# Even rounds of scores and sums, loads in pieces, and one tile for a pair's keys and queries

## The chip, the cores and the metric

The kernel runs on one core of a Trainium2 chip. The metric is the device time of one launch in microseconds (us). Names of engines: PE is TensorE's matmuls and PEld its weight loads, ACT is ScalarE, DVE is VectorE, POOL is GpSimd, SP is SyncE, which here only issues DMA transfers.

## The reference

Sigmoid attention and then a mixture of experts with one expert for each token:

```python
# q, k, v: 8 batches, 12 heads, 448 tokens, 64 wide
scores = (1 / sqrt(64)) * q @ k.T - log(448)
attn   = sigmoid(scores)
x      = attn @ v                      # tokens x 768 after the heads are put side by side
# 3584 tokens, 8 experts of 768 -> 1024 -> 768
logits = x @ w_gate;  e = argmax(logits);  g = softmax(logits)[e]
out    = g * (relu(x @ w1[e]) @ w2[e])
```

There is no softmax over the keys, so the score of each key can be activated and summed by itself.

## The kernel before

**Attention.** Two heads make a pair (`g`, 48 of them, six to a batch), and two pairs are worked on together (`u = g // 2`). The 448 keys are seven chunks of 64. One step `s` is one chunk of two pairs, so there are 168 steps, seven to each `u`. `scores(s)` issues four matmuls of 64 keys by 448 queries, one to each 64x64 quarter of PE (the profile records two passes for each, so eight records), and then two activations on ACT (`squash`, line 748) that write the activated scores to tiles `at`, of which there are eight buffers. Their PSUM tiles (`ps_sc`) are four, two a step. `weighted(s)` issues the four matmuls that sum a chunk's values by its activated scores; the seven chunks of a pair accumulate in one PSUM tile.

**Rounds.** Up to step 70 (`START`) attention runs alone. At each even step the loop at line 940 first issues sums (`weigh_to`), then gating work of earlier batches (`stages_early`), then the token transposes of pairs whose sums are done (`turn_tokens`), then two steps of scores (`score_to`), then the copies of finished pairs (`copy_tokens`). Before the change the sums go up to step s-2, but never over the end of a `u`:

```python
weigh_to(min(s - 1, (done_av // ST + 1) * ST))
```

As a `u` has seven steps and a round has two, the rounds at steps 16, 30, 44 and 58 have one sum, and those at 18, 32, 46 and 60 have three. Step 70 has three. `summed` notes the round in which a `u` was finished; a batch's gate matmuls (`gate_a`, line 289, 128x32 form) follow one round later, when its third `u` is done.

From step 70 on, the MoE's matmuls (128x128 form) are interleaved, and a `u`'s seven steps of scores and sums come as one burst. Order on each engine is the program's (`manual_schedule`).

**Start.** Pairs 0 and 1 are loaded with their rows on the partitions (`load_rows`, line 673), pair 0 from SP and pair 1 from ACT, and transposed on PE (`turn_rows`, line 702) behind a warm-up of 33 matmuls: all seven chunks of the queries of both pairs, then those of the keys, whose first chunk has a PSUM tile of its own so that step 0 can begin early. DVE and ACT copy the results. Pair 3 is loaded in the same way from ACT and transposed on DVE in 32x32 blocks (`turn_blocks`, line 724): eight instructions for its keys and eight for its queries. Pair 2 and all later ones are loaded in pieces of 128 bytes and transposed by one DVE instruction each (`turn`, line 694). Behind pair 3's blocks, DVE makes a constant (line 101) and transposes pair 2. Scores of pairs 2 and 3 begin at step 7.

`blank_records` (line 109) fills a table in DRAM that the later gating writes into: two fills on POOL and one DMA from a tile of the ring `wst`, whose five buffers later hold raw weights.

Of the kernel before, what the change touches and what calls it, by code (L numbers as in the profile page):

```python
# [18 lines left out]
P = 128  # L19
# [5 lines left out]
def tile_sigmoid_attention_top1_moe(  # L25
# [83 lines left out]
    def blank_records():  # L109
        blank = wpool.tile([P, 1024], U32, tag="wst", bufs=RAWS_AHEAD, name="blank")  # L110
        blank3 = blank[:, : E * NT // P * 2].rearrange("p (r w) -> p r w", w=2)
        for w, val in enumerate((int(BIG), 0)):
            nc.gpsimd.iota(blank3[:, :, w], pattern=[[0, E * NT // P]], base=val, channel_multiplier=0)
        nc.gpsimd.dma_start(recs.rearrange("(p r) w -> p r w", p=P), blank3)
# [542 lines left out]
    def load_pair(g):  # L657
# [3 lines left out]
        for nm, src in (("k", k), ("q", q)):  # L661
# [8 lines left out]
                    )  # L670
            ops[g, nm + "n"] = t

    def load_rows(g, nm):

        t = apool.tile([P, KC, D], F32, tag=nm + "n", bufs=4, name=f"{nm}n_{g}")
        src = (k if nm == "k" else q)[0, 2 * g : 2 * g + 2]
        (nc.scalar if g else nc.sync).dma_start(t, src.rearrange("h (p c) d -> (h p) c d", c=KC))
        ops[g, nm + "n"] = t

    def load_values(g):  # L680
        if g >= NG or (g, "v") in ops:
# [39 lines left out]
                if to > at:  # L721
                    copy(t[:, at * DK : to * DK], ps[:, at * DK : to * DK])

    def turn_blocks(g, nm):

        rows = ops.pop((g, nm + "n"))
        t = apool.tile([P, S], F32, tag=nm + "t", bufs=4, name=f"{nm}t_{g}")
        for a in range(0, P, DK):
            for p in (0, 32):
                for d in (0, 32):  # L730
                    nc.vector.transpose(
                        t[a + d : a + d + 32].rearrange("d (c p) -> d c p", c=KC)[:, :, p : p + 32],
                        rows[a + p : a + p + 32, :, d : d + 32],
                    )
        ops[g, nm] = t

    def warm_up(n):

# [79 lines left out]
    START = 70  # L818
    LOADS = (START - 15, START - 12, START - 9, START - 7, START - 5)
    FIRST = (START - 3, START - 1, START - 1)  # L820
    SPLITS = (START - 11, START - 10, START - 9, START - 8, START - 4, START - 3)
    PB = NP // 2 * ST
    MIX = (7, 7)

# [3 lines left out]
        2: lambda u: (turn(2 * u + 3, "k"), load_pair(2 * u + 5)),  # L828
        3: lambda u: (turn(2 * u + 3, "q"), load_values(2 * u + 3)),
    }  # L830
    BURST = 4

    def attention():

        order = ExitStack()
        order.enter_context(tc.manual_schedule())
        make_identity(nc, ident)
        warm_up(WARM)
        for nm in "qk":
            load_rows(0, nm)  # L840
            load_rows(CROSS, nm)
        for n in range(2):
            load_values(n)
        for nm in "kq":
            load_rows(3, nm)
        turn_rows("q", 0)
        turn_rows("k", 1)
        for nm in "kq":
            turn_blocks(3, nm)
        nc.gpsimd.memset(wg, 0.0)  # L850
        nc.gpsimd.dma_start(wg[:, :, :E], w_gate.rearrange("(t p) e -> p t e", p=P))
        setup()
        load_pair(2)
        blank_records()
        for n in (2, 3):
            load_values(n)
        list_constants()
        done_av = done_sc = 0

        def weigh_to(n):  # L860
            nonlocal done_av
            while done_av < min(n, N_ST):
                weighted(done_av)
                done_av += 1

        def score_to(n):
            nonlocal done_sc
            while done_sc < min(n, N_ST):
                scores(done_sc)
                done_sc += 1  # L870

        gate = {}

        def stage(what, b):
            g = gate.setdefault(b, {})
            if what == "B":
                g["oh"], g["z"] = early_b()
            elif what == "C":
                ri, *g["early"] = early_c(g["oh"], g["z"])
                g["c"] = None, None, ri  # L880
            elif what == "C3":
                oh, ce, keep, cnt, sums = g["early"]
                g["lm"] = early_c2(oh, ce, keep, cnt)
                early_c3()
            elif what == "D":
                oh, ce, keep, cnt, sums = g["early"]
                for n in range(2):
                    sl_of[n] = early_d(n, g["lm"][:, n], sums[:, :, n], cnt[:, n * E : (n + 1) * E])
            elif what == "b":
                g["oh"], g["z"] = gate_b(b)  # L890
            elif what == "c":
                g["c"] = gate_c(b, g["oh"], g["z"])
            elif what == "c2":
                g["lm"] = gate_c2(b, g["oh"], *g["c"])
            elif what == "c3":
                gate_c3(b, *g["c"][:2])
            elif what == "l" and b > 0:
                load_slot(b - 1, g["c"][2])
            elif what == "d":
                sl_of[b] = gate_d(b, g["lm"])  # L900
            elif what[0] == "s":
                gate_d2(b, int(what[1]))
            elif what == "g" and b > 0:
                gate_g(b - 1)
            elif what == "e" and b > 0:
                gate_e(b - 1)

        LATE = {8: "b", 10: "c", 11: ("l", "c2"), 12: "c3", 15: "d", 16: "g", 26: "e"}
        FOUR = ("s0", "s1", "s2", "s3")
        PUTS = tuple(dict(zip(range(r, r + 8, 2), FOUR)) for r in (START - PB, START + 10 - 2 * PB)) + 4 * (dict(zip((27, 28, 29, 30), FOUR)),)  # L910
        PUTS += (dict(zip((25, 26, 27, 28), FOUR)), {9: "s0", 10: "s1"})
        LAST = {3: "b", 5: "c", 6: ("l", "c2"), 7: "c3", 8: "d", 9: "g"}
        EARLY = {5: "B", 7: "C", 9: ("l", "C3"), 11: "D", 13: "g", 32: "e"}
        FIRST_LATE = {8: "b", 10: "c", 11: ("l", "c2"), 12: "c3", 15: "d", 16: "g", 26: "e"}
        PLACES = {}
        for b in range(B):
            places = ({}, EARLY, FIRST_LATE, LATE, LATE, LATE, LATE, LAST)[b]
            for r, what in [*places.items(), *PUTS[b].items()]:
                at = (b + 1) * PB + r
                at += at < START and at % 2  # L920
                PLACES.setdefault(at, []).extend((w, b) for w in ((what,) if isinstance(what, str) else what))

        summed = {}

        def stages_early(s):
            for b in range(B):
                if summed.get((b + 1) * NP // 2 - 1) == s - 2:
                    gate_a(b)
            for w in PLACES.get(s, ()):
                stage(*w)  # L930

        def stages_late(s):
            u, i = divmod(s, ST)
            b, r = divmod(s - PB, PB)
            if r == (BURST if b < B - 1 else 1) and (b + 1) * PB >= START:
                gate_a(b)
            for w in PLACES.get(s, ()):
                stage(*w)

        for s in range(N_ST + 11):  # L940
            u, i = divmod(s, ST)
            a = u * ST
            if s in LOADS:
                wts.load(LOADS.index(s) + 1)
            if s in FIRST:
                wts.ahead(FIRST.index(s) + 1)
            if s < START:
                if s % 2 == 0:
                    weigh_to(min(s - 1, (done_av // ST + 1) * ST))
                    if done_av and done_av % ST == 0:  # L950
                        summed.setdefault(done_av // ST - 1, s)
                    stages_early(s)
                    turn_tokens()
                    score_to(s + 2 if s else LEAD + 1)
                    copy_tokens()
            elif s == START:
                weigh_to(a)
                turn_tokens()
                score_to(a + 2)
                copy_tokens()  # L960
            yield s, MIX[0]
            keep_tokens()
            if s >= START:
                b, r = divmod(s - 3 * PB, PB)
                b += 1
                stages_late(s)
                if i == BURST:
                    for n in range(ST):
                        score_to(a + n + 3)
                        weigh_to(a + n + 1)  # L970
                        turn_tokens()
                        if n == ST - 1:
                            copy_tokens()
                        if r == PB - ST + BURST and n < KD:
                            split_tokens(b, n, nc.scalar.copy if n in (1, 4) else nc.vector.tensor_copy)
            if i in READY and s < N_ST:
                READY[i](u)
            if s in SPLITS:
                split_tokens(0, SPLITS.index(s), nc.vector.tensor_copy)
            yield s, MIX[1]  # L980
        keep_tokens()
        order.close()
# [384 lines left out]
```

## Time and profile before

| | us |
|---|---|
| median of 3 runs | 771.38 (771.14 to 772.06) |
| the profiled execution | 771.24, span 769.4 |
| PE busy | 762.8 (99%) |
| ACT, DVE, POOL busy | 382.2, 378.2, 349.1 |
| TensorE's granted clock | 1.00 |

The span runs from the first instruction of the program to the last. PE's busy time says little of how well its four quarters are filled: a matmul counts as busy until its modelled end. The weight loads (PEld) tell when each matmul's turn comes, four to a wave while the 64x64 quarters are in use. A bracket in a timeline row is the engine's idle time before the row and what ended it; "issue" means that the profile shows no one it waited for.

### The profile page before, as it was taken

What the parts mean: (1) busy time and instruction counts of PE and PEld (TensorE: products, weight loads), DVE (VectorE), ACT (ScalarE), POOL (GpSimd) and SP (SyncE); (2) the same over time, 40 slices, a digit from 0 to 9 for tenths busy, and PEclk for the clock granted to TensorE, in tenths of its full rate; (3) what the DMA queues carried; (4) which work ended last, traced back from release to release, by engine and by line L of the source; (5) the groups of instructions that cost most, each with busy time, mean ns of one, the idle gap of its engine ahead of it and who ended that gap; (6) DMA issues with size and microseconds to landing.
All of it is one profiled execution on the core that took longest, in us unless ns stands there. A gap on an engine that the chain in (4) does not pass through costs nothing. (4 is left out here: it accounts for less than half of the span.)

```text
span 769.4 us, 15492 instructions
## 1 busy us (share of the span) xinstructions
PE 762.8 (99%) x5585; PEld 589.3 (77%) x5585; DVE 378.2 (49%) x790; ACT 382.2 (50%) x686; POOL 349.1 (45%) x342
## 2 busy tenths in 40 slices
PE   9999999999999999999999999999999999999997
PEld 5655547678687696876967769678689999999996
DVE  5433678375253751628415474244746392244443
ACT  6878676644526545364344552545523333445451
POOL 8665526245353151531705407044266654764351
PEclk9999999999999999999999999999999999999999
DMA  9786898896678665694575966566087454656671
GB/s 231 166 180 148 177 243 177 189 217 149 157 162 192 147 154 120 160 242 99 134 184 110 218 149 168 129 185 151 24 217 173 142 142 107 204 154 172 199 222 38
DMA packets 309921, 125.67 MB, mean 163 GB/s; under 512 B 208158, under 2 KB 305358, under 8 KB 309840
## 3 DMA queue, kind: packets, MB, share of 16 engines
q1 hardware_dynamic: 303632, 112.19, 61.6%
q0 software_dynamic: 5632, 11.53, 5.4%
q8 instruction: 45, 0.74, 0.5%
q10 hardware_dynamic: 576, 0.92, 0.4%
q14 instruction: 36, 0.29, 0.1%
HBM read 102.49 MB, written 22.49 MB: 162 GB/s over the span
## 5 line engine op out<-in xcount | busy, mean ns | idle before, releaser
L750 ACT ACTIVATE at<-sc,bias_s 128x448 f32<-128x448 f32 x336 | 190.7, 633 | 106.9 <-PE sc L768 106.2
L162 POOL TENSOR_TENSOR w1l<-wst,w1h 128x768 fp32r<-128x768 f32 x72 | 132.8, 1852 | 210.5 <-ACT w1h L161 207.9
L162 POOL TENSOR_TENSOR w2l<-wst,w2h 128x512 fp32r<-128x512 f32 x84 | 106.9, 1296 | 134.7 <-ACT w2h L161 134.6
L768 PE MATMUL sc<-qt,kt 64*64 64x448 f32 x1344 | 162.0, 543 | 0.0
L784 PE MATMUL av<-at,vn 64*64 64x448 f32 x1344 | 160.1, 536 | 0.0
L243 PE MATMUL ps<-xh,w1h 128*128 128x448 f32 x336 | 124.3, 370 | 0.0
L243 PE MATMUL ps<-xh,w1l 128*128 128x448 f32 x336 | 123.3, 367 | 0.0
L243 PE MATMUL ps<-xl,w1h 128*128 128x448 f32 x336 | 123.3, 367 | 0.0
L266 PE MATMUL ps<-hh,w2l 128*128 128x448 f32 x336 | 123.3, 367 | 0.0
L266 PE MATMUL ps<-hl,w2h 128*128 128x448 f32 x336 | 123.2, 367 | 0.0
L266 PE MATMUL ps<-hh,w2h 128*128 128x448 f32 x336 | 122.6, 365 | 0.0
L768 PEld LDWEIGHTS sc<-qt,kt 64*64 64x64 f32 x1344 | 75.3, 188 | 59.0 <-issue 46.5
L784 PEld LDWEIGHTS av<-at,vn 64*64 64x64 f32 x1344 | 57.5, 133 | 64.0 <-issue 53.8
L161 ACT CAST w2h<-wst 128x512 fp32r<-128x512 f32 x108 | 64.5, 620 | 75.7 <-PE ps L266 63.3
L250 ACT ACTIVATE hh<-ps 128x448 fp32r<-128x448 f32 x56 | 30.5, 545 | 138.1 <-PE ps L243 125.3
L279 DVE TENSOR_TENSOR ps<-ps,gt 128x448 f32<-128x448 f32 x42 | 40.7, 970 | 87.0 <-PE ps L266 84.7
L612 DVE STREAM_TRANSPOSE xt<-av 128x448 f32<-128x448 f32 x45 | 26.5, 626 | 95.3 <-PE av L784 95.3
L251 DVE SCALAR_TENSOR_TENSOR hl<-ps,hh 128x448 fp32r<-128x448 f32 x56 | 34.4, 614 | 76.5 <-ACT hh L250 67.0
L243 PEld LDWEIGHTS ps<-xh,w1h 128*128 128x128 f32 x336 | 63.1, 188 | 9.4 <-issue 4.4
L266 PEld LDWEIGHTS ps<-hh,w2l 128*128 128x128 f32 x336 | 65.2, 194 | 6.6 <-issue 3.5
L266 PEld LDWEIGHTS ps<-hl,w2h 128*128 128x128 f32 x336 | 65.2, 194 | 6.2 <-issue 3.2
L266 PEld LDWEIGHTS ps<-hh,w2h 128*128 128x128 f32 x336 | 65.2, 194 | 3.2
(215 smaller groups left out, 916.5 us busy)
## 6 DMA issues: line engine op xcount, KB each, us to landing
wst<-in_moe_w_dram SPq DMA_DIRECT2D x72, 384.0 KB
wst<-in_moe_w_dram SPq DMA_DIRECT2D x54, 512.0 KB
x_tok<-xt SPq DMA_DIRECT2D x64, 168.0 KB
qn<-in_q_dram SPq DMA_DIRECT2D x180, 56.0 KB
raw<-x_tok SPq DMA_DIRECT2D x28, 336.0 KB
out_dram<-ob SPq DMA_DIRECT2D x84, 112.0 KB
kn<-in_k_dram SPq DMA_DIRECT2D x104, 56.0 KB
kn<-in_k_dram POOLq DMA_DIRECT2D x76, 56.0 KB, 4.1
```

The lines of the kernel that those rows point to most:

```text
L161: nc.scalar.copy(hi, st)
L162: eng.tensor_tensor(lo, st, hi.bitcast(F32), op=ALU.subtract)
L243: nc.tensor.matmul(ps[:, :S], a[:, ws], b_, start=(t == 0 and n == 0), stop=(t == KD - 1 and n == 2))
L250: nc.scalar.activation(hh[:, :S], ps[:, :S], AF.Relu)
L251: nc.vector.scalar_tensor_tensor(hl[:, :S], ps[:, :S], 0.0, hh[:, :S].bitcast(F32), op0=ALU.max, op1=ALU.subtract)
L266: nc.tensor.matmul(ps[:, :S], a, b_, start=(j == 0 and n == 0), stop=(j == KF - 1 and n == 2))
L279: nc.vector.tensor_tensor(by_gate, by_gate, gate_rows[b], op=ALU.mult)
L612: nc.vector.transpose(xts[b][:, :, t, :], pv[:, :S].rearrange("p (j s) -> p j s", s=32))
L750: nc.scalar.activation(at, ps[:, :S], AF.Sigmoid, bias=bias_s, scale=SCALE)
L768: nc.tensor.matmul(ps[quarter(g, h), :S], ks, ops[g, "q"][own], start=True, stop=True)
L784: nc.tensor.matmul(psv[g][OWN[1 - h if g == CROSS else h], :S], ops[g, "v"][rows, c, :], at[rows], start=(c == 0), stop=(c == KC - 1))
```

## The change

Five things. (1) Sums go up to step s-3 (`BEHIND = 2`) with no stop at the end of a `u`, so each round from step 4 to step 68 has two sums and step 70 has four; a `u` may now be finished in the middle of a round, and `summed` notes it in that round. (2) `load_rows` issues two transfers for each of the four tiles: chunks 0 to 3 (1024 bytes a partition) and chunks 4 to 6 (768 bytes). (3) Pair 3's keys and queries lie side by side in one tile of the ring `wst`, still one transfer each, both from ACT; their transposes go to a second such tile by eight instructions that each take keys and queries together. (4) `blank_records` is issued at step 14, not at the start. (5) The last of the six splits of the first slot's tokens (`SPLITS`) is at step 68, not 67.

```diff
+    def rows_of(g, nm):
+        return (k if nm == "k" else q)[0, 2 * g : 2 * g + 2].rearrange("h (p c) d -> (h p) c d", c=KC)
+
     def load_rows(g, nm):
         t = apool.tile([P, KC, D], F32, tag=nm + "n", bufs=4, name=f"{nm}n_{g}")
-        src = (k if nm == "k" else q)[0, 2 * g : 2 * g + 2]
-        (nc.scalar if g else nc.sync).dma_start(t, src.rearrange("h (p c) d -> (h p) c d", c=KC))
+        for cs in (slice(0, 4), slice(4, KC)):
+            (nc.scalar if g else nc.sync).dma_start(t[:, cs], rows_of(g, nm)[:, cs])
         ops[g, nm + "n"] = t
+
+    def load_both(g):
+        t = wpool.tile([P, 1024], F32, tag="wst", bufs=RAWS_AHEAD, name=f"kqn_{g}")
+        ops[g, "kqn"] = t = t[:, : 2 * S].rearrange("p (n c d) -> p n c d", n=2, c=KC)
+        for n, nm in enumerate("kq"):
+            nc.scalar.dma_start(t[:, n], rows_of(g, nm))
...
-    def turn_blocks(g, nm):
-        rows = ops.pop((g, nm + "n"))
-        t = apool.tile([P, S], F32, tag=nm + "t", bufs=4, name=f"{nm}t_{g}")
+    def turn_blocks(g):
+        rows = ops.pop((g, "kqn")).rearrange("p n c d -> p (n c) d")
+        t = wpool.tile([P, 1024], F32, tag="wst", bufs=RAWS_AHEAD, name=f"kqt_{g}")[:, : 2 * S]
+        by_c = t.rearrange("d (c p) -> d c p", p=DK)
         for a in range(0, P, DK):
             for p in (0, 32):
                 for d in (0, 32):
-                    nc.vector.transpose(
-                        t[a + d : a + d + 32].rearrange("d (c p) -> d c p", c=KC)[:, :, p : p + 32],
-                        rows[a + p : a + p + 32, :, d : d + 32],
-                    )
-        ops[g, nm] = t
+                    nc.vector.transpose(by_c[a + d : a + d + 32, :, p : p + 32], rows[a + p : a + p + 32, :, d : d + 32])
+        ops[g, "k"], ops[g, "q"] = t[:, :S], t[:, S:]
...
-    SPLITS = (START - 11, START - 10, START - 9, START - 8, START - 4, START - 3)
+    SPLITS = (START - 11, START - 10, START - 9, START - 8, START - 4, START - 2)
...
-    BURST = 4
+    BURST, BEHIND = 4, 2
...
-        for nm in "kq":
-            load_rows(3, nm)
+        load_both(3)
...
-        for nm in "kq":
-            turn_blocks(3, nm)
+        turn_blocks(3)
...
         load_pair(2)
-        blank_records()
...
-                    weigh_to(min(s - 1, (done_av // ST + 1) * ST))
-                    if done_av and done_av % ST == 0:
-                        summed.setdefault(done_av // ST - 1, s)
+                    weigh_to(s - BEHIND)
+                    while len(summed) < done_av // ST:
+                        summed[len(summed)] = s
...
+            if s == 2 * ST:
+                blank_records()
             yield s, MIX[0]
```

## Rows read from the trace of the kernel before

**Rows 1.** The page: busy time, share of the span, instructions.

```profile
PE 762.8 (99%) x5585; PEld 589.3 (77%) x5585; DVE 378.2 (49%) x790; ACT 382.2 (50%) x686; POOL 349.1 (45%) x342
```

**Rows 2.** Timeline of PEld: start, duration, instruction, count, idle before; even stretches.

```profile
88.75 1.35 PEld L768 LDWEIGHTS sc<-qt,kt 64*64 64x64 f32 x16 [0.20 <-issue]
...
96.27 0.17 PEld L784 LDWEIGHTS av<-at,vn 64*64 64x64 f32 x4
...
143.98 0.15 PEld L784 LDWEIGHTS av<-at,vn 64*64 64x64 f32 x4 [0.22 <-issue]
144.84 0.19 PEld L243 LDWEIGHTS ps<-xh,w1h 128*128 128x128 f32 x1 [0.70 <-issue]
```

**Rows 3.** PEld by stretches: window, length, busy (loads), clock, DMA share, GB/s.

```profile
6.45:42.53 36.08, 21.24 (x376) 1.00 0.87 187
43.81:77.48 33.67, 17.26 (x352) 1.00 0.75 161
86.00:110.64 24.64, 12.39 (x256) 1.00 0.98 209
111.91:120.72 8.81, 4.53 (x88) 1.00 0.89 184
134.09:144.83 10.74, 5.00 (x112) 1.00 0.72 147
```

**Rows 4.** Timeline of ACT around step 16.

```profile
27.86 3.98 ACT L750 ACTIVATE at<-sc,bias_s 128x448 f32<-128x448 f32 x7 [0.80 <-PE sc L768]
```

**Rows 5.** Timeline of PEld behind step 16.

```profile
30.32 0.20 PEld L768 LDWEIGHTS sc<-qt,kt 64*64 64x64 f32 x2 [0.21 <-ACT at L750]
30.33 0.14 PEld L784 LDWEIGHTS av<-at,vn 64*64 64x64 f32 x2
```

**Rows 6.** Timeline of PEld at the end of the second stretch.

```profile
76.65 0.14 PEld L784 LDWEIGHTS av<-at,vn 64*64 64x64 f32 x2 [0.24 <-issue]
77.50 0.91 PEld L294 LDWEIGHTS psg<-xf,wg 128*32 128x32 f32 x24 [0.71 <-issue]
```

**Rows 7.** Timeline of the start, SP and PEld.

```profile
1.17 0.44 SPq L677 DMA_DIRECT2D kn<-in_k_dram  x1
...
1.04 3.30 PEld L741 LDWEIGHTS <-ones 128*128 128x128 bf16 x33 [1.04 <-DVE ones L76]
4.55 0.94 PEld L714 LDWEIGHTS turn_q<-ident,qn 64*64 64x64 f32 x56 [0.22 <-issue]
5.54 0.21 PEld L714 LDWEIGHTS sc_first_k<-ident,kn 64*64 64x64 f32 x8
...
6.46 0.21 PEld L768 LDWEIGHTS sc<-qt,kt 64*64 64x64 f32 x8
```

**Rows 8.** All engines by stretches of the start; last columns clock, DMA share, GB/s.

```profile
2.00:4.00 2.00, 2.00 (x21) 2.00 (x20) 0.00 (x0) 0.63 (x2) 2.00 (x6) 1.00 0.87 293
4.00:6.00 2.00, 1.93 (x91) 1.73 (x93) 0.35 (x1) 0.29 (x1) 2.00 (x5) 1.00 1.05 399
6.00:8.00 2.00, 2.00 (x57) 1.02 (x52) 1.76 (x6) 1.36 (x4) 1.69 (x5) 1.00 1.11 311
```

**Rows 9.** Waits of SP's queue up to 10 us: total, times, longest.

```profile
SPq L667 <- DMA qn<-in_q_dram: 1.9, 1, 1.9
```

**Rows 10.** Timeline of DVE behind the start.

```profile
10.44 3.32 DVE L731 STREAM_TRANSPOSE qt<-qn 32x224 f32<-32x224 f32 x8
13.79 0.29 DVE L101 TENSOR_SCALAR upper<-step_i,slot 128x128 bf16<-128x128 f32 x1
...
14.58 0.60 DVE L699 STREAM_TRANSPOSE qt<-qn 128x448 f32<-128x448 f32 x1
```

**Rows 11.** Timeline of ACT: the first activations.

```profile
7.48 4.30 ACT L750 ACTIVATE at<-sc,bias_s 128x448 f32<-128x448 f32 x8 [0.32 <-PE sc L768]
```

**Rows 12.** Timeline of POOL: the blank records' issue, and the idle time before step 16.

```profile
6.93 0.60 POOL L114 DMA_DIRECT2D recs<-blank  x1 [0.30 <-POOL blank L113]
...
29.56 0.57 POOL L687 DMA_DIRECT2D vn<-in_v_dram  x1 [4.56 <-PE av L784]
```

## The prediction, made before the changed kernel was run

> **What bounds the kernel now.** I read the busy table first: TensorE (PE) is busy 762.8 us of a span of 769.4 [rows 1]. So only what moves PE's own idle time can move the end; the other engines, at about half, matter where PE waits for them. The row doesn't show such waits, because a pipelined matmul counts as busy while two of the four tiles stand still. So I went to the weight loads (PEld), each of which begins one matmul. In the attention part PE works as four 64x64 tiles, and four loads make a wave. In an undisturbed stretch 20 waves take from 88.75 to 96.27, or 0.376 us each [rows 2]. One step (scores or sums of two pairs, eight loads) is two waves, 0.752 us.
>
> The stretches table then gives the loss: window, less loads / 4 x 0.376 [rows 3]. Stretch 1 (6.45 to 42.53): 36.08 - 94 x 0.376 = 0.74. Stretch 2 (43.81): 33.67 - 88 x 0.376 = 0.58. Stretch 3 (86.00): 24.64 - 64 x 0.376 = 0.58. Stretch 4 (111.91): 8.81 - 22 x 0.376 = 0.54. A burst after step 70 (134.09): 10.74 - 28 x 0.376 = 0.21. [...] 0.21 is what a stretch pays to fill and drain. The first four lose 0.53 + 0.37 + 0.37 + 0.33 = 1.60 us more. Each of them holds one or two uneven rounds: steps 16; 30 and 44; 58; and at step 70 three sums behind two.
>
> How an uneven round costs: in step 16's round one sum stands where two did, so PE is at its scores 0.75 us sooner, while ScalarE (ACT) is still in seven activations without a pause [rows 4]. Scores have four PSUM tiles, two steps' worth, so they wait for ACT, and PE comes out of it with two tiles in scores and two already in sums [rows 5]. From there one half runs a wave ahead of the other. It costs nothing until the stretch ends: then the last loads come as two, not four, and PE drains half empty. Stretch 2 ends so, with two loads at 76.65; the burst ends with four at 143.98; both then need 0.85 us to the next form of matmul [rows 2, 6]. Half a wave pair late is 0.376 us, which is the 0.33 to 0.37 counted.
>
> **The change, part by part.** *Even rounds.* Every round before step 70 now has two sums, of steps s-4 and s-3 in the running count, so PE spends 1.50 us before each pair of scores, as it does today in the rounds without a loss. Step 70 has four sums; the last one's activations get one sum (0.75 us) more. The matmuls are the same in number. Four steps of activated scores are held instead of three, which is all eight buffers; the slot that is written was freed by a sum two steps of PE's order earlier (sum s-4, sum s-3, scores s), so no wait. The token copies and the values' reloads come up to one round (1.5 us) later for half of the pairs, behind them on GpSimd (POOL) and SyncE (SP) the next keys and queries; these are used seven steps (10.5 us) on. If that cover went, PE would wait for keys by what is over. I take 1.60 us saved of stretches 1 to 4, between 0 (the loss is the drain's own) and 1.60, nearest to the burst's 0.21.
>
> *Loads in two pieces.* Today the queries' transposes start at 4.55, 0.21 after the warm-up's last load ends (1.04 + 3.30), and end at 5.49; the keys' at 5.54, and the first score is at 6.46 [rows 7]. The keys' transposes take 0.92. With pieces, four sevenths of each can be done before the second piece is there, so the order is PE's own: 0.94 + 0.92 from about 4.4 gives 6.26, 0.2 us sooner. Above this the gain could be 0.4 (three sevenths of 0.92 behind the last keys at 5.5, less the copies); below it nothing, if smaller descriptors stretch the stream: 917 KB in four tiles at 399 GB/s [rows 8] take 2.3 us, and a tenth more would eat the 0.2. I take 0.2.
>
> Every DMA issue counts: four more, 0.44 us each on SP, and as many on ACT, which has nothing else to do before the copies at 5.6. What is queued behind them shows on SP: its next transfer waited 1.9 us for the first queries' landing [rows 9]. It is the ninth of SP and ACT together, so eight are in flight and the next waits. Now q and k alone are eight, so the values of pairs 0 and 1 and the fourth pair's loads wait for the first pieces, about 3.8, and flow when the keys are through (0.3 MB of the 917 KB remain at 4.0, so 4.8). The stream has hardly a gap. The values are now needed one round later, behind four steps of scores: 6.26 + 4 x 0.752 = 9.3; that they are there by 8.2 is worked out next.
>
> *Fourth pair in one tile.* Sixteen transposes of 32x224, 0.414 apart (3.32 / 8), become eight of 32x448 [rows 10]. No row has that form. Bounds: 0.60, the whole 128x448 one, and 0.83, twice the small one. I take 0.62, since a transpose of the same elements per partition is nearer than one with two fixed parts. That is 5.0 us instead of 6.6. But all eight now need both loads. From the windows [rows 8]: 1.38 MB by 6.0 (little moves before 2.0), and the 1.84 MB of eight tiles by 7.4 (the last 0.45 MB at 311 GB/s); a landing is told about 0.7 after its last byte (keys: 4.8 by bytes, 5.54 by PE). So 8.1 today, 8.2 with the late issue, and the blocks end at 13.2, where today they end at 13.76. From there to the end of the third pair's queries it is 1.42 (15.18 - 13.76): 14.6.
>
> [...]
>
> PE wants step 7's scores earlier than now: seven scores and four sums after 6.26, so 6.26 + 11 x 0.752 = 14.5 (today 12 steps after 6.46: 15.5). Today the 15.18 is just in time; now 14.6 against 14.5 is a stall of 0.1. ACT adds one: eight activations in 4.30 [rows 11] from 0.2 sooner, 7.28, end at 11.58, and scores of step 5 want their slot at 6.26 + 7 x 0.752 = 11.5, so 0.1. As both estimates err late more than early, I take 0.35 for both; bounds 0 and 2.4 (landing at 9.0, 0.83 each: 9.0 + 6.6 + 1.4 = 17.0, less the 14.5).
>
> *Blank records later.* The issue of 0.60 and its two fills move from 6 to 7.5 us to step 14, about 26 us, where POOL is idle for 4.56 us [rows 12]. 0; without that cover a few keys would be issued 1.5 us later, seven steps ahead of use. *The last split of slot 0* moves one step on; VectorE (DVE) has it done long before the MoE's sixteenth matmul. 0.
>
> **Sum.** -0.20 (start) - 1.60 (rounds) + 0.35 (first rounds' new waits) = -1.45 us. After step 70 the order is the same and PE-bound (the burst above), so it passes to the end. The profiled execution took 771.24 (769.4 and 1.84 around it); it is 0.14 below the median of the runs, 771.38. So 769.93.
>
> **Rivals.** *A, the drain.* The 0.33 to 0.37 could be the cost of going over to gate matmuls of another tile form, which stays. Then only the start is left: -0.20 + 0.35 = +0.15, 771.5. For it: three of the four stretches end in such a switch. Against it: the switch takes 0.85 after the last load either way [rows 2, 6], and a burst that ends in another form too loses 0.21.
> [...]
> *B, the blocks come late (slower).* The fourth pair's blocks wait for the later of two loads that are now issued behind eight pieces, and PE's step 7 waits for DVE. Price at the upper bound 2.4: -1.80 + 2.4 = +0.6, 772.0. It decides from the point where the blocks end after 14.9 (14.5 + 1.8 - 1.42). For it: nothing is spare, 14.6 against 14.5. Against: DVE's work there shrinks by 1.6.
> *C, no new waits.* The first rounds stall nowhere and the start gains 0.4: -2.0, 769.4. For it: DVE is only 0.1 short, by estimates. Against: ACT's eight activations have no pause to give.
> *D, the rounds stay uneven in effect:* ACT, with the weights' casts before step 70, still holds up scores; half of 1.60 comes: 770.7. Against: no round of two shows it.
>
> **Chances and range.** Forecast (769.4 to 770.4) 0.52, A 0.12, B 0.08, C 0.16, D 0.12. A measurement here tells about 0.2%, 1.54 us, from no change, so faster means below 769.84. Of the forecast's 0.52 some 0.24 lies there, with C 0.40. Slower, above 772.92, is only B with more than its price, 0.05. Within: 0.55. The range 769.0 to 771.8 holds A, C and D and most of B's near side.
>
> **What would show it.** Right: excess of each of the four stretches about 0.2 (stretch 1 about 0.55), last loads before the gate in fours, no ACT release in steps 16, 30, 44 and 58; first score at 6.2 to 6.3; eight 32x448 transposes of 0.6. Wrong: stretches that still lose 0.55 with even rounds (A); a PE wait for DVE at 14 to 17 us of over 1 us (B); or a different length from step 70 to the end, which nothing here foresees.

## The result: 6.5 us slower, where 1.5 us faster was forecast

The changed kernel takes 777.98 us (median of 6 runs, 777.64 to 778.70), the kernel before 771.46 beside it (6 runs). The ratio is 1.0085, 95% interval 1.0072 to 1.0098. The forecast of 769.9 failed in sign, and its range (769.0 to 771.8) too. The profiled execution is the slowest of the six: 778.70, span 776.9, so profile against profile the loss is 7.5 us.

The busy line of the changed kernel's page looks like that of before [rows 1], PE at 99% in both; the loss can't be seen there.

```profile
PE 765.7 (99%) x5585; PEld 589.0 (76%) x5585; DVE 376.2 (48%) x782; ACT 383.8 (49%) x686; POOL 349.4 (45%) x342
```

The weight loads by stretches do show it (window, length, busy with loads, clock, DMA share, GB/s; the first window also holds the last eight loads of the keys' transposes, so its own loads are 400):

```profile
7.66:48.67 41.01, 22.07 (x408) 1.00 0.85 176
49.94:80.23 30.29, 14.47 (x320) 1.00 0.72 154
89.24:118.49 29.25, 15.32 (x288) 1.00 0.91 188
119.77:128.33 8.56, 3.47 (x64) 1.00 0.92 182
```

With the prediction's own formula (length less loads / 4 x 0.376) and beside [rows 3]:

| | before | after |
|---|---|---|
| first score at | 6.46 | 7.67 |
| stretch 1 over its waves | 0.74 | 3.41 |
| stretch 2 | 0.58 | 0.21 |
| second gate, first load to next score | 1.27 | 1.81 |
| stretch 3 | 0.58 | 2.18 |
| stretch 4 | 0.54 | 2.54 |
| first MoE load (end of stretch 4) | 120.73 | 128.34 |

The differences are 1.21 + 2.67 - 0.37 + 0.54 + 1.60 + 2.00 = 7.65, against 7.61 between the two MoE starts (the rest is rounding). From there on nothing changes: the last score stretch starts at 543.05 before and at 550.65 after, 7.60 later. So all of it is lost in the first 128 us, and stretch 2 alone went as forecast.

What PE waited for there (total, times, longest):

```profile
PE sc L777 <- DVE qt L710: 1.6, 1, 1.6
PE sc_first_k L725 <- DMA kn<-in_k_dram: 1.3, 1, 1.3
PE sc L777 <- DVE logits L298: 1.3, 1, 1.3
...
PE av L793 <- DMA vn<-in_v_dram: 0.6, 1, 0.6
```

Four single waits, one for each place. I take them in order of time.

**The start.** The timeline of the weight loads (start, duration, instruction, idle before and its releaser), to be held beside [rows 7]: the queries are even a little earlier, the keys 1.3 us later.

```profile
4.47 0.91 PEld L725 LDWEIGHTS turn_q<-ident,qn 64*64 64x64 f32 x56
6.86 0.21 PEld L725 LDWEIGHTS sc_first_k<-ident,kn 64*64 64x64 f32 x8 [1.48 <-DMA kn<-in_k_dram]
7.67 0.21 PEld L777 LDWEIGHTS sc<-qt,kt 64*64 64x64 f32 x8
```

And all engines in the window from 4 to 6 us (last columns clock, DMA share, GB/s), beside [rows 8]: the DMA moves 190 GB/s where it moved 399.

```profile
4.00:6.00 2.00, 1.52 (x63) 1.28 (x61) 0.45 (x1) 0.39 (x1) 2.00 (x5) 1.00 0.92 190
```

**Step 7.** ACT's queue issues the fourth pair's two loads at 3.31 and 3.75, and DVE has to wait for the later one; the eight blocks (0.65 each) begin at 11.37, and the third pair's queries, behind them, end at 17.96. PE is back at 18.08. First DVE, then PEld:

```profile
11.37 5.18 DVE L743 STREAM_TRANSPOSE kqt<-kqn 32x448 f32<-32x448 f32 x8 [2.87 <-DMA kqn<-in_q_dram]
...
17.36 0.60 DVE L710 STREAM_TRANSPOSE qt<-qn 128x448 f32<-128x448 f32 x1
```

```profile
18.08 0.23 PEld L777 LDWEIGHTS sc<-qt,kt 64*64 64x64 f32 x2 [2.38 <-ACT at L759]
```

The releaser named here is ACT; the matmuls' own list above names DVE's queries (1.6), which had ended just before.

**Values of pair 17.** POOL's queue stands for 7.19 us at the even pair's values, whose tile comes free with the later sums, and the odd pair's values leave behind four key loads at 95.20 (before: 89.28). The 336 KB load of the slot's tokens left on SP's queue at 93.58, so ahead of them. PE stands 1.36 at those values. POOL, then PEld:

```profile
92.09 0.58 POOL L698 DMA_DIRECT2D vn<-in_v_dram  x1 [7.19 <-PE av L793]
92.66 2.55 POOL L667 DMA_DIRECT2D kn<-in_k_dram  x4
95.20 1.07 POOL L702 DMA_DIRECT2D vn<-in_v_dram  x2
```

```profile
104.39 0.19 PEld L793 LDWEIGHTS av<-at,vn 64*64 64x64 f32 x2 [1.36 <-DMA vn<-in_v_dram]
```

**The third gate.** It now comes at step 68, not 66, and so behind the split at step 66 in DVE's order. DVE waits 3.15 for queries, then does the queries, the whole split, and only then the copy that empties the gate's PSUM tile, which is one of the four score tiles:

```profile
118.68 0.65 DVE L710 STREAM_TRANSPOSE qt<-qn 128x448 f32<-128x448 f32 x1 [3.15 <-DMA qn<-in_q_dram]
119.25 0.60 DVE L594 STREAM_TRANSPOSE whole<-raw 128x448 f32<-128x448 f32 x1
119.89 1.96 DVE L595 CAST xh<-whole 128x448 fp32r<-128x448 f32 x1
121.89 0.62 DVE L598 TENSOR_TENSOR xl<-whole,xh 128x448 fp32r<-128x448 f32 x1
122.43 0.38 DVE L298 COPY logits<-psg 128x224 f32<-128x224 f32 x1
```

```profile
122.86 0.20 PEld L777 LDWEIGHTS sc<-qt,kt 64*64 64x64 f32 x2 [2.03 <-DVE logits L298]
```

The order alone does not make the 2.03: the cast in this split took 1.96 us, not the 0.39 of before, beside a product on POOL (last section). Without the 1.57 more, an estimated 0.46 would be left here.

In the kernel before the copy stood ahead of that split, and of the queries, and came as soon as the gate ended:

```profile
112.06 0.39 DVE L298 COPY logits<-psg 128x224 f32<-128x224 f32 x1 [1.29 <-PE psg L294]
```

### The profile page after: what moved, and what is told of

Same layout as the page of the kernel before. It is cut to its first block, busy times and chain, and to the rows that moved or that the text cites. A ratio compares the mean times of both kernels' runs of the same rounds, so it can differ in the third digit from the quotient of the medians.

```text
span 776.9 us, 15491 instructions
## 1 busy us (share of the span) xinstructions
PE 765.7 (99%) x5585; PEld 589.0 (76%) x5585; DVE 376.2 (48%) x782; ACT 383.8 (49%) x686; POOL 349.4 (45%) x342
```

## The experiments

Theory: the sums' extra lag delays what hangs on them (token copies, gate, values' tiles) inside queues that are worked in order, and the pieces delay the keys. Rivals: the pieces alone; the one tile; the evening itself.

### The change taken apart

**The lag alone (e1):** the kernel before with the new rounds and the moved last split.

```
-                    weigh_to(min(s - 1, (done_av // ST + 1) * ST))
+                    weigh_to(s - BEHIND)   # BEHIND = 2
...
-    SPLITS = (START - 11, START - 10, START - 9, START - 8, START - 4, START - 3)
+    SPLITS = (START - 11, START - 10, START - 9, START - 8, START - 4, START - 2)
```

> The kernel before with the sums one step later alone (and the last split at step 68); loads, fourth pair and blank records as before. Theory L (the later sums push what is queued behind them in order on DVE, POOL and in PSUM): the start stays at 6.46 and step 7 does not wait, the second stretch has no excess, but the waits of the changed kernel for values (1.4 us near 103), for the logits copy (2.0 near 121) and for a pair's queries (0.65 near 30) come again in part: 772 to 774. Rival S (all of the loss is the start's, the later waits follow from it): excess of all stretches gone, 769.9 to 770.3.

775.86 us, ratio 1.0055 (1.0038 to 1.0072): 4.4 of the 6.5 us. Its stretches, the second left out:

```profile
6.78:46.06 39.28, 21.15 (x400) 1.00 0.87 180
...
86.34:115.09 28.75, 15.42 (x288) 1.00 0.96 195
116.36:124.92 8.56, 3.40 (x64) 1.00 0.95 188
```

Over their waves 1.68, (0.21,) 1.68 and 2.54: stretch 4 loses what it loses in the whole change, stretch 3 most of it, stretch 1 half. The time is above the 772 to 774 of its theory L. PE does wait at step 7, with all loads whole, and again at step 14:

```profile
15.47 0.34 PEld L768 LDWEIGHTS sc<-qt,kt 64*64 64x64 f32 x8 [0.85 <-ACT at L750]
27.79 0.72 PEld L768 LDWEIGHTS sc<-qt,kt 64*64 64x64 f32 x10 [0.70 <-ACT at L750]
```

**The pieces alone (e2):** two transfers a tile for pairs 0 and 1.

```
-        (nc.scalar if g else nc.sync).dma_start(t, src...)
+        for cs in (slice(0, 4), slice(4, KC)) if g < 2 else (slice(0, KC),):
+            (nc.scalar if g else nc.sync).dma_start(t[:, cs], rows[:, cs])
```

> The kernel before with the first two pairs' queries and keys in two pieces alone. Theory S: the keys land late (last near 7.2), first score at 7.6 instead of 6.46, and the fourth pair's loads land after 9, so PE waits near step 7: 773 to 775. Rival (the pieces are harmless, the fourth pair's single tile or the absent blank records did it): first score 6.2 to 6.5, 771.2 to 771.6.

772.81, ratio 1.0015 (1.0005 to 1.0024): 1.36 slower. The gain of 0.2 that the prediction took is a loss; the keys' first matmul waits 0.72 for its load and the first score is at 7.12. The stream moves 261 GB/s between 4 and 6 us.

```profile
6.31 0.21 PEld L716 LDWEIGHTS sc_first_k<-ident,kn 64*64 64x64 f32 x8 [0.72 <-DMA kn<-in_k_dram]
```

**The one tile alone (e3):** `load_both` and the new `turn_blocks`, all loads whole.

```
-        for nm in "kq":
-            load_rows(3, nm)
+        load_both(3)
...
-        for nm in "kq":
-            turn_blocks(3, nm)
+        turn_blocks(3)
```

> The kernel before with the fourth pair's keys and queries in one tile and eight transposes alone. Theory S: loads issue at 1.6 and 2.1 as before, land by 8.5, eight transposes of 0.65 end at 13.7, nothing waits: 771.2 to 771.6, first score 6.46. Rival (the single tile makes step 7 late): PE waits over 0.5 us for DVE near 15, 772 or more.

771.62, ratio 1.0 (0.999 to 1.0009): nothing, for or against. Its eight transposes begin when both loads are there (8.48) and end at 13.67, where the sixteen end at 13.76.

**Even rounds without the extra lag (e4):** the new rounds, but the sums one step behind the scores, uncapped.

```
-                    weigh_to(min(s - 1, (done_av // ST + 1) * ST))
+                    weigh_to(s - BEHIND)   # BEHIND = 1
```

> The kernel before with the sums up to step s-2 in each round and no stop at the end of a u: even rounds without one step more of lag. Theory L: the excess of stretches 2 and 3 (0.37 each) goes and no new wait comes: 770.2 to 770.7. Rival (the excess is the drain's own): 771.3 to 771.6, stretches 2 and 3 still at 0.58.

771.38, ratio 0.9997 (0.9988 to 1.0007). The first two stretches:

```profile
7.29:42.79 35.50, 17.62 (x376) 1.00 0.87 177
44.30:77.62 33.32, 17.57 (x352) 1.00 0.75 162
```

Over their waves 0.16 and 0.23 (0.74 and 0.58 before), the third 0.23 as well, so the prediction's reading of the uneven rounds holds: rival A (the drain's own cost) falls. Why the time of this execution stays: each of the three gates takes 1.51, not 1.27, since the gate's matmuls come at ACT's second token copy before it is done, and the first score was 0.84 later. That last is not the change: the queries' 56 transposes took 1.59 us in this execution and 0.94 in that of before, with the same program up to there. Stretches and gates together are 0.56 better; the interval of the medians (0.9 us faster to 0.5 slower) can neither show nor exclude that. The gate:

```profile
77.63 1.15 PEld L294 LDWEIGHTS psg<-xf,wg 128*32 128x32 f32 x24 [0.70 <-issue]
```

Stretch 4 stays at 0.53 here, since step 70 still has three sums behind two; with the lag it has four (e11 below: 0.22).

### Which queue it is

**The gate's copy ahead of the late splits (e5):** e1 with both late splits after step 68.

```
-    SPLITS = (START - 11, START - 10, START - 9, START - 8, START - 4, START - 2)
+    SPLITS = (START - 11, START - 10, START - 9, START - 8, START - 2, START - 1)
```

> The later sums alone, as in e1, but the last two splits of slot 0 (DVE transpose, cast and subtraction) stand behind the third gate's logits copy instead of one before it. Theory L: PE's wait of 2.0 us for that copy goes, the fourth stretch's excess falls from 2.3 to under 0.4, the rest of e1 stays (775.86): 773.6 to 774.2. Rival (the copy is late by itself, behind the wait for a pair's queries, or the MoE's first matmuls then wait for the splits instead): 775.3 to 776.

773.85, ratio 1.0033 (1.0019 to 1.0046): 2.0 less than e1. DVE now copies the logits right behind the queries, and the last stretch loses 0.57 (6.59 - 16 x 0.376), not 2.54:

```profile
116.96 0.65 DVE L699 STREAM_TRANSPOSE qt<-qn 128x448 f32<-128x448 f32 x1 [3.06 <-DMA qn<-in_q_dram]
117.53 0.35 DVE L298 COPY logits<-psg 128x224 f32<-128x224 f32 x1
```

```profile
116.81:123.40 6.59, 3.11 (x64) 1.00 0.82 168
```

**Pieces without the gate weights' load among them (e6):** e2 with the load of 768 rows of 32 bytes on POOL's queue issued later, and a memset of equal place on POOL.

```
-        nc.gpsimd.dma_start(wg[:, :, :E], w_gate...)
+        nc.gpsimd.memset(idle, 0.0)
...
         list_constants()
+        nc.gpsimd.dma_start(wg[:, :, :E], w_gate...)
```

> Pieces alone, as in e2, but the gate weights' load (768 rows of 32 bytes from POOL) is issued behind the other early loads, and a fill keeps POOL busy in its place. Theory W (its small rows come between the keys' pieces and slow the DMA engines): the keys' last piece lands near 5.5 and the first score is at 6.2 to 6.5. Rival P (the pieces themselves, or the transfers waiting behind them, slow the stream): keys land at 6.4 to 7.2 as in e2, first score at 7.1 or later.

773.23 (one run). The first score comes at 6.97, with 0.54 of waiting for the keys (0.72 in e2). The small rows were at most a small part of the cause.

**Pieces by head (e7):** e2, but each half is 64 partitions with the whole 1792-byte row.

```
-            ...dma_start(t[:, cs], rows[:, cs])
+            ...dma_start(t[ps], rows[ps])     # ps: partitions 0 to 63, 64 to 127
```

> Two transfers a tile as in e2, but cut by head: 64 partitions of 1792 bytes each instead of 128 partitions of 1024 and 768. Theory D (the size of the rows): the stream keeps 400 GB/s, keys land by 5.5, first score at 6.3 to 6.6. Rival N (the number of transfers, eight before the first waits): keys land at 6.4 to 7.2, first score at 7.0 or later.

774.37 (one run). The keys land between 6.12 and 8.18, later than in e2 (5.88 to 6.69). So whole rows do not bring the stream back. That the shorter rows cost nothing in e2 doesn't follow: e7's transfers span half the partitions, and SP takes 0.58 to 0.60 to issue one, where it takes 0.41 to 0.44 in e2 and before. What in the cut transfers slows the stream stays open; that less was on its way behind them was not tried either (the values leave SP's queue at 3.51 in e2 and at 1.66 before).

### Making the evening pay

**Even rounds, one tile, and the second pair's token copy on DVE (e8):** e3 and e4 together, and

```
-                nc.scalar.copy(xf, pv[:, :S])
+                (nc.vector.tensor_copy if g % 2 and g < 20 else nc.scalar.copy)(xf, pv[:, :S])
```

> Even rounds without the extra step (as e4), the fourth pair in one tile (as e3), and up to step 70 each round's second token copy on DVE instead of ACT. In e4 the three gates took 0.24 us longer each, as PE waited there for ACT's second copy. Theory L: stretches 1 to 3 without excess and gates of 1.27 us: 1.2 to 1.5 us under the kernel before, 769.9 to 770.3. Rival (the copies delay DVE's transposes, or the gates wait for something else): 771 or more.

771.09 (11 runs) against 771.56 (16 runs), ratio 0.9997 (0.9988 to 1.0006): no difference that can be told. The trace, of the fastest of the eleven executions, has what was expected of the attention part, stretches of 0.29, 0.23, 0.23 and 0.53 and gates of 1.27, 1.27 and 1.28. Its first and last stretch:

```profile
6.36:41.99 35.63, 26.18 (x376) 1.00 0.89 189
...
110.66:119.46 8.80, 4.55 (x88) 1.00 0.90 194
```

The MoE starts at 119.47, 1.26 sooner, and the last score stretch too (541.79); the span is 0.8 shorter (768.6). Of the other 0.46, 0.28 goes near 550, at the last sums, where PE stands 0.33 for ACT. It is the best version tried, not a proven gain.

### What is left of the lag

**The slot's token load later (e9):** e5 with that load two steps later in the program, the splits two to three.

```
-        EARLY = {5: "B", 7: "C", 9: ("l", "C3"), 11: "D", ...
+        EARLY = {5: "B", 7: "C", 9: "C3", 11: ("l", "D"), ...
-    SPLITS = (START - 11, START - 10, START - 9, START - 8, START - 2, START - 1)
+    SPLITS = (START - 8, START - 7, START - 6, START - 5, START - 2, START - 1)
```

> The lag alone, both late splits behind the third gate's copy, and the slot's 336 KB token load two steps later (with the splits moved two to three steps later), so that it is issued behind the values of the second pair of that round and not ahead of them. Theory V (that the values came late because of the raw load ahead of them in the shared DMA engines): the attention-only stretch before the third gate, 1.47 us over its floor in the lag kernel with the splits behind the gate, falls to 0.25 (-1.2), the rest stays, median 772.6. Rival (the values are late because their tile comes free a round later, whatever is ahead of them): 1.2 or more stays, 773.8. Rival (the split's tokens become the late ones): the wait moves into the last stretch or the first slot's products, 774 or above.

773.99, ratio 1.0028 (1.0017 to 1.0039): as e5. But the edit did not move the load: SP issued it at 91.35 in e5 and at 90.86 here, both times behind SP's read of the slot's number, for which SP's queue waits on DVE (3.4 us in the kernel before, 3.7 in the changed one). So this run says nothing on the values; stretch 3 keeps 1.65.

**The whole change with whole loads (e10):**

```
-        for cs in (slice(0, 4), slice(4, KC)):
-            (nc.scalar if g else nc.sync).dma_start(t[:, cs], rows_of(g, nm)[:, cs])
+        (nc.scalar if g else nc.sync).dma_start(t, rows_of(g, nm))
```

> The whole change, but the first two pairs' queries and keys loaded whole: lag, one tile with eight blocks and the later blank records stay. Theory P (pieces are what makes the changed kernel slower than the lag alone): first score at 6.4 to 6.8 instead of 7.67, first stretch 1.7 over its floor instead of 3.43, the gates as in the lag alone, median 775.9 (the lag alone had 775.86). Rival (the one tile or the later blank records cost 0.5 or more beside the lag): 776.5 to 778.

776.21, ratio 1.0058 (1.004 to 1.0076). So the pieces cost 1.77 in the whole change (777.98 - 776.21), and lag, tile and blank records together 0.35 more than the lag alone, which the runs can't tell from none (the later blank records were never run alone). The profiled execution is the slowest of the four (777.23): in it the fourth pair's queries landed at 10.26, not at 8.25 as in e8, and DVE's blocks and step 7 were late as in the changed kernel. Here the cast in the split took 0.40, but the queries ahead of it came 1.6 later against the gate than in the changed kernel, and PE stood as long at the same copy.

```profile
10.36 5.19 DVE L742 STREAM_TRANSPOSE kqt<-kqn 32x448 f32<-32x448 f32 x8 [3.55 <-DMA kqn<-in_q_dram]
```

```profile
121.32 0.19 PEld L776 LDWEIGHTS sc<-qt,kt 64*64 64x64 f32 x2 [2.08 <-DVE logits L298]
```

**The same with e9's edits (e11):**

> The whole change with three edits against its three causes: queries and keys whole, both late splits behind the third gate's copy, the slot's token load two steps later. If the lag's cost was only those places: 775.9 - 2.0 (splits) - 1.2 (values) = 772.7, still above the kernel before by the first stretch (1.1 us more over its floor than before) and the gates (+0.25 each). Rival (something else of the change costs): 774 or above.

774.82, ratio 1.0042 (1.0027 to 1.0057), where 772.7 was expected. 1.2 of the miss is e9's edit, which moves nothing (stretch 3 keeps 1.72). Stretch 4 came down to 0.22 (6.24 - 16 x 0.376), all that can be had. Stretch 1 keeps 2.69: PE waits 1.1 for the third pair's queries even in this execution, the quickest of the five, where the fourth pair's queries landed at 9.04. Before step 7's loads PE is idle 1.85, where e1, without the tile, has 0.85. Of the 1.00 more, 0.63 is that the first score came sooner (6.16, in e1 6.79) and 0.38 that the queries were done later (15.73, in e1 15.35); so this is mostly the lag, which wants those scores a step earlier, and the later landing, for which all eight blocks of the one tile wait, adds the smaller part. In e10 and e11 POOL, with no blank records to write at 6 us, issues its next key loads, three and four, from 6.82 on, not from 8.41; whether that is what delays the landing was not tried.

**The odd pair's values ahead of the next keys (e12):** e5 with the order on POOL's queue changed.

```
-        2: lambda u: (turn(2 * u + 3, "k"), load_pair(2 * u + 5)),
-        3: lambda u: (turn(2 * u + 3, "q"), load_values(2 * u + 3)),
+        2: lambda u: (turn(2 * u + 3, "k"), load_values(2 * u + 3), load_pair(2 * u + 5)),
+        3: lambda u: turn(2 * u + 3, "q"),
```

> The lag alone with both late splits behind the third gate's copy, and the values of each round's second pair issued on their queue ahead of the four key loads of the pair after, not behind them (in the lag kernel they leave at 93.0 and 93.5 us, behind four key issues of 0.63 and behind the slot's token load of 91.35 to 93.3, and land at 101.3 and 101.8). Theory V (that place in the queues is what makes the values late): they leave by 91.5, land by 98, the attention-only stretch before the third gate falls from 1.47 over its floor to 0.25, median 772.6. Rival (the shared DMA engines are full there anyway, so that something else is late by as much, the keys first): 1 us or more of it stays, 773.6 or above. Of the lag's cost that would leave the first stretch (some 1.6 over its floor) and the gates.

772.84, ratio 1.0016 (1.0007 to 1.0026): 1.0 less than e5. POOL's queue and stretches 3 and 4:

```profile
89.97 0.57 POOL L687 DMA_DIRECT2D vn<-in_v_dram  x1 [6.62 <-PE av L784]
90.53 1.06 POOL L691 DMA_DIRECT2D vn<-in_v_dram  x2
91.59 5.05 POOL L667 DMA_DIRECT2D kn<-in_k_dram  x8
```

```profile
87.11:114.76 27.65, 13.13 (x288) 1.00 0.93 194
116.03:123.26 7.23, 3.43 (x64) 1.00 0.87 193
```

The values leave at 90.53, ahead of the token load, and land by 94.72. Stretch 3 loses 0.58, in e5 1.45. No wait of PE for the keys, up to 1.2 us later, shows. But stretch 4 loses 1.21, in e5 0.57: the third gate is 0.78 sooner, the queries that stand ahead of its copy on DVE come only 0.13 sooner, and PE waits for the copy again.

```profile
116.83 0.65 DVE L699 STREAM_TRANSPOSE qt<-qn 128x448 f32<-128x448 f32 x1 [3.45 <-DMA qn<-in_q_dram]
```

```profile
117.80 0.20 PEld L768 LDWEIGHTS sc<-qt,kt 64*64 64x64 f32 x2 [0.69 <-DVE logits L298]
```

So the traces show the place, but little net gain: this execution (773.80, near the slowest of the ten) and that of e5 (773.85) take the same time. The 1.0 rests on the medians of ten runs and five. The edit took the values ahead of the key issues and of the token load at once; which of the two counts, it can't say.

## Why the prediction was wrong

The step that failed is the passage on the lag's side effects: "The token copies and the values' reloads come up to one round (1.5 us) later for half of the pairs, behind them on GpSimd (POOL) and SyncE (SP) the next keys and queries; these are used seven steps (10.5 us) on." It named one thing that stands behind the late ones, the next keys and queries, and measured it by its slack. It did not ask the same of the odd pair's values, which stand behind those keys, of the gate, or of anything on DVE, and so put the lag's waits there at nothing. Of the 6.5 us, by medians:

- **Gate and DVE's order, 2.0** (e1 to e5). The prediction named the copies and the reloads but not the gate, which is started by the sums too and moved from step 66 to 68, past a split. It costed the splits at nothing because their result is used late; what counted is that a copy which frees a score tile stood behind one, and that the cast in that split took 1.96 us, five times the 0.39 of before.
- **Values on POOL's queue, 1.0** (e5 to e12). The odd pair's reload left 5.9 us later in the changed kernel (95.20 for 89.28), but there PE itself was 3.2 late by then (stretch 3 begins at 89.24, before at 86.00). Against PE's own place it is 2.7 late, and 2.7 in e5 too (92.97, stretch 3 from 87.02), where the prediction had 1.5. It stands behind four key issues and the wait for the even pair's tile, and the token load now leaves before it.
- **The rest of the lag, 1.3** (e12 against before). In e12's trace stretch 1 loses 1.19 more than before, stretch 4 0.67 more and the second gate 0.26, and stretch 2 gives 0.37 back. Stretch 1's two places are the same in every trace with the lag: step 7 (PE idle 0.85 to 1.09 in e1, e5, e9 and e12, where 0.2 before a load is usual), and step 14 (0.70 to 0.71 in all), where the token copies and transposes of pairs 0 and 1 on DVE, now a round later, stand ahead of the queries of pair 5. No run took these two places away. DVE at step 14 of the change, where PE goes on at 30.41:

```profile
27.17 0.65 DVE L612 STREAM_TRANSPOSE xt<-xf 128x448 f32<-128x448 f32 x1 [6.76 <-ACT xf L820]
27.82 1.26 DVE L818 COPY xf<-av 64x448 f32<-64x448 f32 x2
29.12 0.65 DVE L612 STREAM_TRANSPOSE xt<-xf 128x448 f32<-128x448 f32 x1
29.69 0.60 DVE L710 STREAM_TRANSPOSE qt<-qn 128x448 f32<-128x448 f32 x1
```

In the kernel before the same work of DVE begins at 21.50, and pair 5's queries are done by 25.67.

- **Pieces, 1.4 to 1.8** (e2; after less e10), forecast as a gain of 0.2. The prediction saw the risk in the right place ("if smaller descriptors stretch the stream") and bounded it at nothing lost, though it had itself worked out that eight transfers would be in flight and that the others would wait. It took the stream's rate from whole loads; that rate fell from 399 to 190 GB/s (261 in e2). The waiting itself came as worked out: SP's fifth and ACT's fifth transfer leave at 3.47 and 3.31. What was wrong is that the stream would have "hardly a gap".
- **Step 7**, where pieces and lag meet. Rival B named this mechanism, with an upper bound of 2.4 from a landing at 9.0; PE stood 2.38, with the landing at 11.27. That the two numbers agree is chance: the bound has blocks of 0.83 each (0.65 measured), a first score at 6.26 (7.67 measured), and its own sum, 17.0 less 14.5, gives 2.5. B got 0.08 because the landing was worked out with the unbroken stream. Where the loads are whole and there is no lag (e3, e8), the landing is at 8.25 to 8.38, near the forecast 8.1, and nobody waits.

The amounts add to 5.7 to 6.1 of the 6.5; the rest is within the spread of the runs.

What held: the uneven rounds cost 0.33 to 0.53 a stretch (0.58, 0.35 and 0.35 back in the first three of e4, 0.37 in stretch 2 of the change, 0.32 in stretch 4 of e11); PE passes a loss on to the end (7.60 of 7.61 in the change, though of e8's gain of 1.26 the span shows 0.8); eight 32x448 transposes take 0.65 each with their gaps (5.18 / 8; taken 0.62); the tile alone changes nothing. What was missing even there: at a gate the evened rounds meet ACT's token copy and give 0.24 back each (e4), so the 1.60 was never to be had whole without moving a copy (e8).

Rival A, the cost of going over to matmuls of another tile form, is not what was lost here: in e4 stretch 2 came down from 0.58 to 0.23 and still ends in such a switch (64x64 to 128x32), and in e8 the gate behind it takes 1.27 as before.

## What to carry to other kernels

When work is moved later, list what each engine and each DMA queue has behind it in its own order, down to copies that only free a buffer; the slack at the use of the next keys and queries (10.5 us) said nothing about those here (2.0 us at the gate's copy, 1.0 at the odd pair's values). Cut in two, this kernel's first loads moved 190 and 261 GB/s between 4 and 6 us (the changed kernel and e2) where whole ones moved 399: take the rate of cut transfers from a row of such transfers, or bound it from below. Where PE goes by a fixed wave, as here by one of 0.376 us, count loads and compare stretch by stretch; the busy share of 99% stood before and after.

## What the runs showed of the hardware that was not expected

- Two halves of the same tiles, together with the values and the fourth pair, moved 190 GB/s (the changed kernel), 261 (e2) and 192 (e7) between 4 and 6 us, where whole tiles moved 399 (before) and 375 (e3).
- VectorE's cast of 128x448 in a split took 0.39 to 0.43 us where no product ran on POOL (105.41 and 107.05 in the kernel before, 106.85 to 111.81 in the changed one). Twelve of them, in ten of the traces between 115 and 124 us, began while POOL's product of 128x768 ran and 0.2 us or more before its end, and each ended 0.24 to 0.26 us behind that product, however early it had begun: it took 1.96 in the changed kernel (119.89 to 121.85, the product 119.79 to 121.60) and in e1, 2.00 in e2, 2.02 and 1.75 in e3, 1.90 and 1.75 in e4, 1.34 in e6 and e8, 0.97 in e11, 0.54 in e9 and 0.45 in e5. A cast that began before the product (118.96 in the kernel before, the product at 119.08) took 0.40. Transposes beside the same product were not longer (0.62 at 117.80 in e5). No run took the product away.
- The start differs between executions by what no edit made: the same 56 transposes of the queries took 0.91 to 0.94 us in nine of the traces, 1.12 in e1, and 1.59 in e4, e5 and e12, where the first score came at 7.29 to 7.31 and not at 6.12 to 6.79 as in the others with whole loads; the granted clock of the window from 4.0 to 5.5 us reads 1.00 in all. Times within 0.8 us of each other were therefore compared by stretches.
